# A written-out order for five queues, redone after the planner's count of instructions for a memory step is corrected

## The chip, the cores and the metric

The kernel runs on one core of a Trainium2 chip. Its time is the device time of one execution in microseconds (us); lower is better. The runs shown before the change took 269.98, 270.18 and 270.83 us.

## The reference

The inputs are bf16; sequence 2048, width 512, 32 heads of 16, four segments of 512 tokens, a feed-forward width of 1792.

```
g = sigmoid((x * gate_w).sum(-1))                       # one gate for each token
a: q, k, v = x@wq, x@wk, x@wv ; for each segment s of 512 tokens:
     p     = softmax(q_s k_s^T / 4 + causal mask);  a_dot = p v_s
     a_mem = phi(q_s) M / (phi(q_s) z + 1e-6)           # what earlier segments left
     o_s   = sigmoid(beta) * a_mem + (1 - sigmoid(beta)) * a_dot
     M += phi(k_s)^T v_s ;  z += sum of phi(k_s)        # phi(t) = t+1 if t>0 else exp(t)
   a = o @ wo
b: h = relu(x@W_gate) * (x@W_up);  b = h @ W_down
out = g * a + (1 - g) * b
```

## The kernel before, in words

The program has no loop at run time. A Python object, `Plan`, holds some 1,100 *steps*; each is a handful of instructions on one engine, with the steps it comes after. A list of numbers, `ORDER`, says what stands in each of five queues: TensorE (PE), ScalarE (ACT), VectorE (DVE), GpSimd (POOL) and SyncE's DMA queue (QSP). An entry v means step v//5 on engine v%5, so the list also chooses the engine where a step may run on two. `Plan.lay_out` walks the queues with costs written in the source and emits the steps in the order of the start that it works out. Each engine then runs its queue strictly in order. The same walk hands out the four PSUM banks `rb0`..`rb3`: a step that needs a bank takes the one that is free earliest.

The steps that are spoken of below; the first digit behind a name is the segment (0 to 3), the next a block of 128 columns (eight heads), a fill or a tile of 128 tokens:

- `Q`, `K`, `V` (L492, L518, L535): projections of a segment, four 128x128 by 512 matmuls each (`V` in two halves of 256). `QC`, `KC`, `VC` (L388/L390) bring them out of PSUM. `KO` (L505/L507) is a masked copy of K.
- `QK` (L751): 8 or 16 short matmuls of scores for one of nine fills of a pair of blocks, into `sp`, which has only one buffer. `EX` (L762, ACT): the exponential of it into one of eleven `E` tiles. `MK` (L772, POOL): the causal mask on it. The next `QK` needs the `EX` before it to be done.
- `PV` (L799): 64 short matmuls for one block, into two banks. `TA`, `N0`, `N1`, `N2`, `TB` (L817, L822, L825, L828, L844, all DVE): transpose out of PSUM, normalise, transpose back into `oT`.
- `EK`, `MN`, `PK`, `KX` (L624, L630, L634, L351): phi of K, then a DMA transpose. `MZ` (L648): the *memory visit*, which adds a segment to M and z: 4 groups x 4 tiles x 4 heads = 64 matmuls of 34 columns, each with its weight load. `MA`, `MB` (L658/L660, L666/L669): into the memory matrix. There are three of them.
- `EQ`, `MQ`, `PQ` (L560, L567, L571): phi of Q. `MR` (L694): reading from the memory, 2 or 3 matmuls. `RA`, `RB`, `RC`, `RN` (L704 to L714, DVE): normalise it. `MX` (L351): a DMA transpose into `memT`. `OA` (L850, DVE or POOL): adds `memT` to `oT`.
- `G`, `U` (L910): gate and up projection of 128 columns, four matmuls each; `R` (L922 on ACT, L924 on DVE): relu; `H` (L929, DVE): product.
- `D`, `DB` (L944, L868) and `W` (L957, L876): the two halves of the down projection and the output projection of 128 tokens in one bank, seven, seven and four matmuls. `W` needs all four `OA` of its segment. `OS` and `ST`: scale and store.
- `XT` (L351): x of a segment, transposed by DMA. `VS` (L465): a shifted copy of V, by DMA. The weights wg, wu come in four pieces by DMA (L339).

TensorE runs in four kinds of array split ("full", "rows", "cols", "cols2"); the walk adds `SWITCH` to a step whose kind differs from the one before. It also counts TensorE's instructions. `CODE` holds the count for a kind of step (a matmul is two: weight load and matmul); others are given where the step is made. Each `PAGE` = 256 of them, from `PAGE0` on, the walk lets TensorE wait, if need be, for the next piece of program:

```
for i in (edge - AHEAD, edge):
    if code <= i < code + s.code:
        t = now + cost * (i - code) / s.code
        if i < edge:
            ask = t
        else:
            cost += max(0.0, asked + FETCH - t)
            asked, edge = max(ask, asked + FETCH), edge + PAGE
code += s.code
```

Of the kernel before, what the change touches and what calls it, by code (L numbers as in the profile page):

```python
# [14 lines left out]
D = 512  # L15
# [17 lines left out]
NWARM = 19  # L33
# [5 lines left out]
SWITCH = 0.094  # L39
ENGINES = ('PE', 'ACT', 'DVE', 'POOL', 'QSP')  # L40
ORDER = [
# [60 lines left out]
]  # L102
T0, TU, SPAN, PEN_D, PEN_A, PEN_P = 19.0, 15.6, 4.1, -23.0, 150.0, 146.0


PORT = {'TG', 'RN', 'RC', 'OA', 'KO', 'MB', 'MQ', 'MN', 'GS', 'PQ', 'PK', 'N1', 'N2', 'N3', 'NM'}
CODE = {'WM': 2 * NWARM, 'XP': 4, 'VI': 2, 'YP': 4, 'D': 14, 'DB': 14, 'PV': 128, 'MZ': 96}
PAGE, PAGE0, AHEAD, FETCH = 256, 186, 12, 5.0
PIECE = {'MK': 0.445, 'TL': 0.22, 'ZE': 0.24, 'YL': 0.22, 'MB': 0.3}


# [910 lines left out]
```

## Time and profile before

| | |
|---|---|
| median of three runs | 270.18 us (269.98 to 270.83) |
| profiled execution, its own time | 270.55 us |
| its span in the trace | 268.8 us |
| outside the span | 1.75 us |
| granted TensorE clock | 1.00 |

The page lists how long each engine was busy; the chain of waits goes back from the last instruction to what released it; the timeline lists an engine's instructions with their start, their duration and, in brackets, the idle time ahead of them. A matmul's listed duration overlaps the next one's, so its price is read from starts: the distance from one start to the next.

### The profile page before, as it was taken

The page shows a single profiled execution, that of the slowest core. Times are in us where ns is not written, and L with a number is a line of the kernel's source. Part 1 is how long each engine was busy: PE and PEld are TensorE (multiplying, and loading weights), DVE is VectorE, ACT ScalarE, POOL GpSimd, SP SyncE. Part 2 cuts the span into 40 slices and gives each one's busy share as a digit, 9 for nine tenths or more (in the row PEclk, how much of TensorE's full clock was granted, in tenths as well). Part 3 has the DMA queues.
Part 4 walks back from the last instruction along what each step waited for, and adds up shares of the span by engine and source line. Part 5 has one row for each costly group of instructions (what it writes and reads, how often), then busy time and mean ns, then how long its engine had stood idle before and what let it go on. Part 6 is the DMA issues. An engine that isn't in the chain of part 4 may idle for free.

```text
span 268.8 us, 8007 instructions
## 1 busy us (share of the span) xinstructions
PE 261.6 (97%) x3337; PEld 124.0 (46%) x3337; DVE 187.4 (70%) x460; ACT 188.6 (70%) x180; POOL 146.3 (54%) x322
## 2 busy tenths in 40 slices
PE   7999999999999998999999998999999999999995
PEld 5444345445444444444444444544544454445453
DVE  1798677988975859898881268886975549465901
ACT  3597878899578696798766886879685577755011
POOL 7047764476978535484753637467558434444110
PEclk9999999999999999999999999999999999999999
DMA  6999176130022321102701010110002130010011
GB/s 191 300 260 247 23 196 221 24 79 2 2 44 76 83 42 22 22 20 41 127 4 39 22 41 2 26 36 0 5 0 67 36 84 2 0 22 0 2 32 49
DMA packets 33422, 16.77 MB, mean 62 GB/s; under 512 B 20074, under 2 KB 33386, under 8 KB 33386
## 3 DMA queue, kind: packets, MB, share of 16 engines
q1 hardware_dynamic: 33098, 16.00, 23.5%
q8 instruction: 26, 0.43, 0.7%
q10 hardware_dynamic: 288, 0.26, 0.3%
q14 instruction: 10, 0.08, 0.1%
HBM read 8.26 MB, written 2.10 MB: 39 GB/s over the span
## 4 chain that ended last, share of the span: by engine, by line
PE 90%; DVE 5%; issue 1%; DMA 1%; ACT 1%; DVEq 0%
PE rb L910 33%; PE rb L944 17%; PE rb L492 10%; PE sp L751 9%; PE rb L799 6%; PE rb L957 5%; PE rb L535 4%; PE rb L518 2%; PE rb L868 1%; PE rb L694 1%; DMA xT<-in_A_x_dram 1%; DVE pqT L571 1%; DVE hT L929 1%; ACT E L762 1%; PE rb L405 1%
## 5 line engine op out<-in xcount | busy, mean ns | idle before, releaser
L772 POOL TENSOR_SCALAR_AFFINE_SELECT E<-E 64x256 bf16<-64x256 bf16 x256 | 113.4, 443 | 98.9 <-ACT E L762 87.3
L762 ACT ACTIVATE E<-sp 128x2048 bf16<-128x2048 f32 x72 | 135.1, 1876 | 40.2 <-PE sp L751 35.8
L910 PE MATMUL rb<-xT,wg_sb 128*128 128x512 bf16 x224 | 55.9, 380 | 1.2 <-DVE o L828 1.2
L910 PE MATMUL rb<-xT,wu_sb 128*128 128x512 bf16 x224 | 56.7, 380 | 0.0
L929 DVE TENSOR_TENSOR hT<-rb,rg 128x512 bf16<-128x512 f32 x56 | 37.8, 681 | 16.5 <-PE rb L910 11.6
L944 PE MATMUL rb<-wd_sb,hT 128*128 128x512 bf16 x210 | 49.0, 379 | 0.0
L910 PEld LDWEIGHTS <-wg_sb 128*128 128x128 bf16 x224 | 20.3, 98 | 26.5 <-issue 5.6
L910 PEld LDWEIGHTS <-wu_sb 128*128 128x128 bf16 x224 | 20.4, 98 | 24.6 <-issue 3.5
L751 PE MATMUL sp<-QT,KTo 32*64 32x512 bf16 (+7 forms) x512 | 30.9, 295 | 0.3 <-issue 0.3
L751 PE MATMUL sp<-QT,KT 16*64 16x512 bf16 (+7 forms) x512 | 30.9, 295 | 0.1
L944 PEld LDWEIGHTS <-hT 128*128 128x128 bf16 x210 | 19.7, 98 | 22.7 <-issue 1.8
L922 ACT ACTIVATE rg<-rb 128x512 bf16<-128x512 f32 x31 | 18.5, 597 | 9.3 <-PE rb L910 7.4
L817 DVE STREAM_TRANSPOSE tA<-rb 128x512 f32<-128x512 f32 x32 | 21.0, 690 | 4.3 <-PE rb L799 4.2
L751 PEld LDWEIGHTS <-KT 16*64 16x64 bf16 x512 | 10.8, 102 | 26.4 <-issue 25.7
L924 DVE TENSOR_SCALAR rg<-rb 128x512 bf16<-128x512 f32 x25 | 16.9, 680 | 4.8 <-PE rb L910 4.6
L799 PE MATMUL rb<-E,Vs 64*32 64x448 bf16 (+7 forms) x512 | 18.0, 284 | 0.0
L799 PE MATMUL rb<-E,Vp 64*32 64x448 bf16 (+7 forms) x512 | 17.5, 283 | 0.0
L492 PE MATMUL rb<-xT,wq_sb 128*128 128x512 bf16 x64 | 16.2, 380 | 0.0
L492 PE MATMUL rb<-xT,wk_sb 128*128 128x512 bf16 x64 | 15.7, 380 | 0.0
L957 PE MATMUL rb<-wo_sb,oT 128*128 128x512 bf16 x60 | 15.1, 379 | 0.0
L828 DVE TENSOR_TENSOR o<-tA,co 128x256 bf16<-128x256 f32 x32 | 14.4, 474 | 0.1
L390 DVE CAST KT<-rb 128x512 bf16<-128x512 f32 x10 | 6.9, 689 | 10.8 <-PE rb L492 10.4
(99 smaller groups left out, 296.3 us busy)
## 6 DMA issues: line engine op xcount, KB each, us to landing
out_dram<-osb SPq DMA_DIRECT2D x15, 128.0 KB, 1.7
wd_sb<-in_B_W_down_dram SPq DMA_DIRECT2D x1, 1792.0 KB
wg_sb<-in_B_W_gate_dram SPq DMA_DIRECT2D x3, 512.0 KB, 6.9
wu_sb<-in_B_W_up_dram SPq DMA_DIRECT2D x3, 512.0 KB, 6.8
Vs<-Vp SPq DMA_DIRECT2D x8, 144.0 KB, 2.6
wk_sb<-in_A_wk_dram SPq DMA_DIRECT2D x2, 256.0 KB, 4.5
wq_sb<-in_A_wq_dram SPq DMA_DIRECT2D x2, 256.0 KB, 5.1
wo_sb<-in_A_wo_dram SPq DMA_DIRECT2D x1, 512.0 KB, 8.4
```

Of the source, the lines that this page charges most:

```text
L492: nc.tensor.matmul(rb[s.bank][:], lhsT=w[:, ci, c * P:(c + 1) * P], rhs=xT[i][:, ci, :], start=(ci == 0), stop=(ci == NC - 1))
L751: nc.tensor.matmul(sp[64 * h:64 * h + 64, j, off:off + m], lhsT=kt[32 * j:hi, c0 + w, 64 * ck:64 * ck + 64], rhs=QT[i][32 * j:hi, c0 + w, ...
L762: nc.scalar.activation(Er[n % NE][:], sp[:], ACT.Exp, scale=SCALE)
L772: nc.gpsimd.affine_select(out=v, in_=v, compare_op=ALU.is_ge, fill=0.0, base=0, pattern=[[0, 4], [1, 64]], channel_multiplier=-1)
L799: nc.tensor.matmul(rb[s.banks[h]][32 * j:32 * j + 32, q0:q0 + m], lhsT=v[64 * h:64 * h + 64, ck // 2, o:o + 32], rhs=Er[(base + f) % NE][6 ...
L817: nc.vector.transpose(tA[k].rearrange("p b w -> p (b w)"), rb[a.banks[r]][:])
L910: nc.tensor.matmul(rb[s.bank][:], lhsT=w[:, ci, fv * P:(fv + 1) * P], rhs=xT[i][:, ci, :], start=(ci == 0), stop=(ci == NC - 1))
L922: nc.scalar.activation(rgb[k][:], rb[a.bank][:], ACT.Relu)
L924: nc.vector.tensor_scalar(rgb[k][:], rb[a.bank][:], 0.0, None, ALU.max)
L929: nc.vector.tensor_tensor(hT[:, fv, :], rb[a.bank][:], rgb[k][:], ALU.mult)
L944: nc.tensor.matmul(rb[b][:], lhsT=hT[:, fv, lc:lc + P], rhs=wd_sb[:, fv, :], start=(fv == 0), stop=False)
L957: nc.tensor.matmul(rb[hold.bank][:], lhsT=oT[i][:, ci, lc:lc + P], rhs=wo_sb[:, ci, :], start=False, stop=(ci == NC - 1))
```

## The change

Two lines of constants and the whole of `ORDER`. No step is added or removed and no instruction is written differently.

```diff
-CODE = {'WM': 2 * NWARM, 'XP': 4, 'VI': 2, 'YP': 4, 'D': 14, 'DB': 14, 'PV': 128, 'MZ': 96}
-PAGE, PAGE0, AHEAD, FETCH = 256, 186, 12, 5.0
+CODE = {'WM': 2 * NWARM, 'XP': 4, 'VI': 2, 'YP': 4, 'D': 14, 'DB': 14, 'PV': 128, 'MZ': 128}
+PAGE, PAGE0, AHEAD, FETCH = 256, 188, 6, 4.6
 ORDER = [
-    135, 81, 79, 140, 150, 170, 146, 160, 157, 176, 350, 167, 355, 375, 360, 365, 380, 372, 190, 180, 385, 197, 390,
+    135, 81, 79, 140, 160, 150, 146, 170, 167, 156, 350, 177, 355, 375, 360, 365, 380, 372, 190, 180, 385, 196, 390,
...
```

The constants act on the kernel only through the walk: the order in which the steps are emitted and the banks that they get. `MZ` is now counted with its 128 instructions. The sets of steps on TensorE and on SyncE's queue are the same as before; eight `R`, and one or two steps each of other kinds, stand on another engine (`R`: 31 on ACT and 25 on DVE before, 23 and 33 now; in all ACT has 170 steps for 179, DVE 428 for 420, POOL 95 for 94).

**TensorE, the third memory visit.** Before, `MZ2` (L648) follows the second `PV` (L799) of the first pair of segment 2 at once, and the next scores (L751) follow it:

```order
L799 LDWEIGHTS Vs_108
L799 MATMUL rb_64<-E_110,Vs_108 32x512
L648 LDWEIGHTS pK
L648 MATMUL rb_65<-Vp_106,pK 32x34
...
L751 LDWEIGHTS KT_101
L751 MATMUL sp<-QT_99,KT_101 64x192
```

In the change a `G` (L910) stands behind that `PV`, and `MZ2` behind scores of segment 3, ahead of a down projection (L944):

```order
L799 LDWEIGHTS Vs_108
L799 MATMUL rb_64<-E_110,Vs_108 32x512
L910 LDWEIGHTS wg_sb
L910 MATMUL rb_65<-xT_97,wg_sb 128x512
...
L751 LDWEIGHTS KTo
L751 MATMUL sp<-QT_100,KTo 64x448
L648 LDWEIGHTS pK
L648 MATMUL rb_67<-Vp_106,pK 32x34
...
L944 LDWEIGHTS hT
L944 MATMUL rb_65<-wd_sb,hT 128x512
```

`MZ2` has moved from instruction 4177 of TensorE's queue to 5153, about 1000 instructions later. The second `PV` with `MZ1` and a `QK` behind it stand together in both kernels, but start at instruction 2463 before and 2425 now.

**VectorE, the first pair of segment 0.** Before, from the first transpose out of PSUM (`TA`, L817) on:

```order
L817 STREAM_TRANSPOSE tA_156<-rb_67 128x512
L817 STREAM_TRANSPOSE tA_157<-rb_65 128x512
L822 RECIPROCAL co_158<-tA_156 128x16
L822 RECIPROCAL co_159<-tA_157 128x16
L825 TENSOR_TENSOR co_158<-co_158,Gs_154 128x16
L825 TENSOR_TENSOR co_159<-co_159,Gs_154 128x16
L828 TENSOR_TENSOR o_0_160<-tA_156,co_158 128x16x16
L828 TENSOR_TENSOR o_0_160<-tA_157,co_159 128x16x16
L817 STREAM_TRANSPOSE tA_156<-rb_66 128x512
```

In the change a `PQ` (L571) and an `H` (L929) stand between:

```order
L817 STREAM_TRANSPOSE tA_156<-rb_65 128x512
L817 STREAM_TRANSPOSE tA_157<-rb_67 128x512
L822 RECIPROCAL co_158<-tA_156 128x16
L822 RECIPROCAL co_159<-tA_157 128x16
L825 TENSOR_TENSOR co_158<-co_158,Gs_154 128x16
L571 SCALAR_TENSOR_TENSOR pqT<-QT_100,e1q_141 128x512
L828 TENSOR_TENSOR o_0_160<-tA_156,co_158 128x16x16
L929 TENSOR_TENSOR hT<-rb_67,rg_146 128x512
L817 STREAM_TRANSPOSE tA_156<-rb_64 128x512
```

Between the first `TA` of blocks 0 and 1 and the first `TA` of blocks 2 and 3 of segment 0, VectorE had 38 steps and now has 44: two `PQ`, two `KO`, one each of `R`, `PK`, `MN`, `MQ` and `GS` came in; one `H`, the `MA` and the `MB` went out.

**SyncE's queue, x of segment 3.** Before, the transposing load of x for segment 3 (`XT3`, into `xT_98`) stands between the two `VS`:

```order
L351 DMA_TRANSPOSE pK<-pkT_145 128x4x128
L465 DMA Vs_108<-Vp_106 64x4x288
L351 DMA_TRANSPOSE xT_98<-in_A_x_dram 128x4x512
L465 DMA Vs_108<-Vp_106 64x4x288
L971 DMA out_dram<-osb_150 128x512
```

Now it stands ahead of the last `MX` (`memT`) of segment 1:

```order
L351 DMA_TRANSPOSE memT<-mtok 128x4x128
L351 DMA_TRANSPOSE pK<-pkT_144 128x4x128 x2
L351 DMA_TRANSPOSE xT_98<-in_A_x_dram 128x4x512
L351 DMA_TRANSPOSE memT<-mtok 128x4x128
L465 DMA Vs_108<-Vp_106 64x4x288 x2
```

That `MX` now comes behind a load that is four times its size, and every `W` of segment 1 comes behind it.

118 rows, old and new, of the table ORDER are left out of this document.

## The prediction

> **What bounds the kernel now.** I read the page first, for which engine carries the time: busy shares, the chain of waits, the DMA queues.
>
> ```profile
> PE 261.6 (97%) x3337; PEld 124.0 (46%) x3337; DVE 187.4 (70%) x460; ACT 188.6 (70%) x180; POOL 146.3 (54%) x322
> q8 instruction: 26, 0.43, 0.7%
> PE 90%; DVE 5%; issue 1%; DMA 1%; ACT 1%; DVEq 0%
> ```
>
> TensorE (PE) is busy 97% of the span and 90% of the chain is its own work; the other engines are busy 70% or less. The change leaves TensorE's steps as they are, and I counted the changes of array split on the two orders: 152 in both. So the change can only win what TensorE loses between its matmuls, and can only lose by making it wait. The second line matters for that: TensorE has 3337 matmuls and as many weight loads, 6674 instructions, and queue q8 fetched 26 blocks of program: one for every 257 instructions.
>
> Next the timeline of TensorE, for breaks in its stream. From segment 1 on there are four that are longer than a quarter of a microsecond:
>
> ```profile
> 105.27 0.29 PE L751 MATMUL sp<-QT,KTo 32*64 32x320 bf16 x1
> 106.78 0.39 PE L910 MATMUL rb<-xT,wg_sb 128*128 128x512 bf16 x1 [1.21 <-DVE o L828]
> ...
> 162.14 0.58 PE L648 MATMUL rb<-Vp,pK 128*32 128x34 bf16 x54
> 163.59 0.25 PE L648 MATMUL rb<-Vp,pK 128*32 128x34 bf16 x10 [0.87 <-issue]
> 163.77 0.27 PE L751 MATMUL sp<-QT,KT 16*64 16x192 bf16 x1
> ...
> 191.48 0.27 PE L751 MATMUL sp<-QT,KT 16*64 16x192 bf16 x1
> 192.07 0.24 PE L751 MATMUL sp<-QT,KTo 32*64 32x192 bf16 x1 [0.32 <-issue]
> ...
> 221.78 0.29 PE L751 MATMUL sp<-QT,KT 16*64 16x320 bf16 x1
> 222.07 0.29 PE L751 MATMUL sp<-QT,KTo 32*64 32x320 bf16 x1
> ```
>
> Three fall in the middle of one step, where no step waits for another. How far apart are they? A count of TensorE's matmuls in the stretches from one break to the next:
>
> ```profile
> 106.50:162.60 56.10, 55.70 (x767) 1.00 0.19 39
> 163.50:191.60 28.10, 28.01 (x384) 1.00 0.08 16
> 192.00:221.85 29.85, 29.78 (x384) 1.00 0.17 43
> ```
>
> 768 (767 and one at the edge), 384 and 384 matmuls: 6, 3 and 3 times 128, which is 256 instructions. All four breaks therefore lie on the seams of the blocks that q8 fetches: TensorE waits for its program. The trace puts the first one down to VectorE (L828), but the bank that this L910 takes was free long before: the transposes (L817) that read it last were over at 104.92.
>
> ```profile
> 103.61 1.31 DVE L817 STREAM_TRANSPOSE tA<-rb 128x512 f32<-128x512 f32 x2 [0.53 <-PE rb L799]
> ```
>
> **What the breaks cost.** By starts, with rows of undisturbed steps beside them:
>
> ```profile
> 222.08 0.32 PE L751 MATMUL sp<-QT,KTo 32*64 32x320 bf16 x1
> 222.33 0.39 PE L910 MATMUL rb<-xT,wu_sb 128*128 128x512 bf16 x1
> ...
> 104.53 0.68 PE L648 MATMUL rb<-Vp,pK 128*32 128x34 bf16 x64
> 105.14 0.27 PE L751 MATMUL sp<-QT,KT 16*64 16x192 bf16 x1
> ```
>
> First: 106.78 - 105.27 = 1.51, less the usual 222.33 - 222.08 = 0.25, is 1.26. Second: `MZ2` takes 163.77 - 162.14 = 1.63, `MZ1` 105.14 - 104.53 = 0.61, so 1.02. Third: 0.59. Fourth: 0.29. The sum is **3.16 us**.
>
> The Trainium skill (Runtime: NRT & Kernel Launch, section "Instruction fetch mechanics") says that an engine's program is refilled in blocks of 16 KiB or 256 instructions, and that a crossing is "one DMA tail-bump, mostly hidden". The trace agrees with the block and with "mostly" (22 of 26 show no such break), not with the four. By the Trainium skill alone the change would win nothing; that is a rival below.
>
> **Why they arise, and whether they go.** A block lasts as long as TensorE takes for its 128 matmuls. For the third and the fourth break, the rows in which the block before it began, counting 128 matmuls back:
>
> ```profile
> 189.30 0.25 PE L799 MATMUL rb<-E,Vp 64*32 64x64 bf16 x8
> 218.53 0.25 PE L799 MATMUL rb<-E,Vp 64*32 64x64 bf16 x8
> ```
>
> Both lie in a `PV` (so do the other two). From there to the resumption it took 192.07 - 189.30 = 2.8 and 222.07 - 218.53 = 3.5 us; the other two lie between. So the next block is there 2.8 to 3.5 us after the present one was entered, and a block that is worked off sooner ends in a break. Only `PV`, `MZ` and `QK` are that dense. The plan before counted each `MZ` 32 instructions short, so that its seams slid off the real ones after each visit; all four breaks come after the first visit.
>
> In the changed order I counted the seams from the same phase and priced the blocks with these starts:
>
> ```profile
> 13.90 1.90 PE L910 MATMUL rb<-xT,wg_sb 128*128 128x512 bf16 x8
> 15.64 1.03 PE L910 MATMUL rb<-xT,wu_sb 128*128 128x512 bf16 x4
> 16.60 0.24 PE L751 MATMUL sp<-QT,KT 16*64 16x128 bf16 x1
> 102.37 0.21 PE L799 MATMUL rb<-E,Vs 64*32 64x64 bf16 x4
> ```
>
> A full matmul is (15.64 - 13.90)/8 = 0.217; a `QK` 0.38 (105.14 to 105.27 and the usual 0.25), with 0.09 for the change of split ahead of it (16.60 - 15.64 - 4 x 0.217); a pair of `PV` 104.53 - 102.37 = 2.16, some 1.0 and 1.16. The shortest block of the new order ends in the second `PV` of segment 3: ten full matmuls, one `QK`, a whole `PV` and 38 of 64 matmuls of the next: 2.17 + 0.47 + 1.0 + 0.69 = 4.3 us. The next shortest, at a `PV` of segment 0 and one of segment 1, come to 4.5 and 4.7 in the same way. `MZ2` stands alone, far from any `PV`; the group with `MZ1` has moved by 38 instructions, so that its second seam falls behind the scores into projections. 4.3 is above 3.5: **all four breaks go, -3.16**. Were a fetch 4.6 us late, as the plan assumes, two short breaks would stay, 0.3 + 0.1 = 0.4.
>
> **What the new order may cost.** *VectorE in segment 0.* The densest stretch of VectorE, from the first `PV` of segment 0 to its third:
>
> ```profile
> 44.90:65.00 20.10, 20.10 (x352) 9.42 (x344) 17.94 (x45) 17.45 (x17) 11.34 (x25) 1.00 0.16 35
> ...
> L571 DVE SCALAR_TENSOR_TENSOR pqT<-QT,e1q 128x512 bf16<-128x512 bf16 x12 | 8.6, 716 | 1.0 <-POOL e1q L567 1.0
> L507 DVE TENSOR_SCALAR KTo<-KT,mcol_o 128x512 bf16<-128x512 bf16 x9 | 3.6, 404 | 0.1
> L924 DVE TENSOR_SCALAR rg<-rb 128x512 bf16<-128x512 f32 x25 | 16.9, 680 | 4.8 <-PE rb L910 4.6
> 53.06 1.09 DVE L666 TENSOR_TENSOR mem<-mzacc,bdm 128x128 bf16<-128x128 f32 x4
> 54.08 0.39 DVE L669 TENSOR_TENSOR mem<-mzacc,bdm 128x32 bf16<-128x32 f32 x1
> ```
>
> Its third number is VectorE: 17.94 busy of 20.10. In come two `PQ` and a `PK`, the same operation on the same shape, 3 x 0.716 = 2.15; two `KO`, and `MQ` and `MN`, which are of `KO`'s kind and shape, 4 x 0.404 = 1.62; an `R` 0.68: 4.45. Out go the `MB`, 1.09 + 0.39, and an `H`, which is as long as the `R`: 2.16. `GS` and `MA`, one short step each, I set off against each other. Net +2.3, against 20.10 - 17.94 = 2.2 of idle time: VectorE is full there. Queued behind it are steps that give banks back (`TA`, `H`, `VC`, `KC`), and TensorE waits for those. It costs between 0, if all of it fits into the idle time, and 2.3, if none does. I take **+0.5**, nearer the lower end: idle time and addition all but cancel, and TensorE has three other banks to work on while one is late; but a queue without gaps cannot make up for a late product.
>
> *Steps that change the engine.* Eight `R` go from ACT to VectorE, 8 x 0.68 = 5.4 us of its 187.4. Outside the stretch above VectorE has room (70% busy over the span), and ACT gets shorter: 0, in the worst case a rival below.
>
> *SyncE's queue.* `XT3` now stands ahead of the last `MX` of segment 1.
>
> ```profile
> 128.99 3.06 SPq L351 DMA_TRANSPOSE xT<-in_A_x_dram  x1
> DMA to landing us min/median/max: 2.4/2.4/4.4
> L850 POOL TENSOR_TENSOR oT<-oT,memT x6: 1154/1157/1382, 117.2 to 256.0; 128x512 bf16<-128x512 bf16 x6
> ```
>
> `XT3` may start after the last `U` of segment 1; then 3.06 on the queue, at most 4.4 for the `MX` (second row), two `OA` on POOL at 1.38: 10.2 us, until the first `W` of segment 1. TensorE has 42 matmuls of `D` and `DB` (9.1) and four `QK` (1.9) in between: 11.0. Cost 0, bounded by 0.5 for a mask that POOL does first. Where this cover is gone, `W` waits for the excess, us for us.
>
> *The rest.* The weight pieces are asked for in another order, but their first readers are moved with them; head and tail have the same steps, and the last `W` is again behind the last block's chain. 0, bounded by 0.3 either way.
>
> **Sum.** Against the profiled execution's own 270.55: -3.16 + 0.5 = 267.9. The median of the runs, 270.18, lies 0.37 lower: **267.5 us**. About 0.3% (0.8 us) is what a measurement of this kernel can tell from no change.
>
> **Rivals.** (1) *The stretch costs its upper end*: VectorE gives banks back late, +2.3 in place of 0.5: 269.7, on the runs' scale 269.3. For it: VectorE is full there. Against: nearly as full before, without a wait. Chance 0.17, split evenly between faster and same. (2) *The breaks are not fetches, or come back at other seams*: 270.2, give or take 0.8. For it: the trace puts one break down to VectorE. The Trainium skill's sentence on the crossing (Runtime: NRT & Kernel Launch, "Instruction fetch mechanics") speaks for it too. Against: distances of exactly 128 matmuls. Chance 0.08, nearly all same. (3) *Slower: VectorE becomes the bound.* If of the 5.4 us of moved `R` nothing fits beside other work, TensorE waits for their banks and the time is 270.55 - 3.16 + 5.4 = 272.8, or 272.4; it decides from 4.0 us on (3.16 and the 0.8), three quarters of it. Against: VectorE is idle for 30% of the span, and many of the moved steps are not near a full stretch. Chance 0.12. The forecast has 0.63, with a range of its own from 266.5 to 268.7.
>
> The range: 266.4 is all breaks gone, no cost and 0.6 of small waits gained; upwards it takes in rival 1 and most of rival 2: 270.0. Faster: 0.63 + 0.09 + 0.03 = 0.75; slower 0.12; same 0.13.
>
> **What would show it.** Right: no idle time of 0.3 us or more put down to "issue" in `MZ`, `PV` or `QK` of PE, and 128-matmul blocks of 4.3 us and more; PE's busy share up by a point. The second step is wrong if breaks of 0.3 us or more recur at multiples of 128 matmuls; the VectorE term if TensorE waits for L817, L929 or L390 between 46 and 68 us by more than 2 us; the SyncE term if a `W` (L957) waits for L850 near 140. The forecast fails if TensorE's waits outside the seams grow by over 2.4 us.

## The result, and the profile after

The changed kernel takes 267.94 us (median of six runs, 267.33 to 268.09), the kernel before 270.36 us beside it (six runs, 269.98 to 270.83). The ratio is 0.9905, with a 95% interval of 0.989 to 0.992: faster by 2.4 us. The forecast was 267.5 us. The profiled execution of the changed kernel took 267.33 us, its span 265.6 us.

The page of the changed kernel, busy times and the chain's shares:

```profile
PE 257.4 (97%) x3298; PEld 123.1 (46%) x3337; DVE 195.3 (74%) x468; ACT 183.9 (69%) x171; POOL 150.6 (57%) x323
PE 96%; issue 2%; DMA 1%; DVE 0%; DVEq 0%
```

VectorE is busier by 7.9 us and ScalarE less busy by 4.7, in the direction of the moved steps, and TensorE still carries the chain. This trace holds 3298 of TensorE's 3337 matmuls (all weight loads are there), so the busy time of PE cannot be compared to the tenth, and some gaps are only missing records. The table of TensorE's waits has to be read with that:

```profile
PE rb L395 <- DVE zeros L267: 1.0, 1, 1.0
PE rb L799 <- issue: 0.9, 1, 0.9
PE rb L944 <- issue: 0.6, 4, 0.2
PE rb L957 <- issue: 0.3, 2, 0.2
```

The two lower rows are gaps of 0.2 us where a full matmul's record is missing; they do not recur in the profiles of this kernel that have all records. The second row is a real break, and a new one. The four of before are gone. In TensorE's timeline (start, duration, engine, line, operation, and in brackets the idle time ahead), the `MZ1` with the `QK` behind it, then `MZ2` at its new place:

```profile
101.60 0.68 PE L648 MATMUL rb<-Vp,pK 128*32 128x34 bf16 x64
102.21 0.27 PE L751 MATMUL sp<-QT,KT 16*64 16x192 bf16 x1
...
102.34 0.29 PE L751 MATMUL sp<-QT,KTo 32*64 32x320 bf16 x1
102.57 1.68 PE L910 MATMUL rb<-xT,wu_sb 128*128 128x512 bf16 x6
...
203.04 0.67 PE L648 MATMUL rb<-Vp,pK 128*32 128x34 bf16 x64
```

From the last score matmul to the next projection (here of `U`) it is 0.23 us, where before it was 1.51, and `MZ2` runs in one piece of 64 where before it was 54, a break, and 10.

The new break lies in the second `PV` of segment 0 (`PV01`, in the first pair):

```profile
42.10 1.90 PE L910 MATMUL rb<-xT,wu_sb 128*128 128x512 bf16 x8
...
46.38 0.39 PE L799 MATMUL rb<-E,Vs 64*32 64x256 bf16 x8
46.50 0.30 PE L799 MATMUL rb<-E,Vp 64*32 64x320 bf16 x1
47.70 0.35 PE L799 MATMUL rb<-E,Vp 64*32 64x320 bf16 x7 [0.91 <-issue]
47.73 0.52 PE L799 MATMUL rb<-E,Vs 64*32 64x384 bf16 x8
```

By starts it lasts 47.70 - 46.50 = 1.2 us, again in the middle of a step. Its price is 1.1 us: from 46.50 to the next row it is 1.23, and 0.14 in the undisturbed step that experiment 3 shows (46.75 to 46.89). Counted back from it, 128 matmuls begin with the second of the eight at 42.10, at about 42.3: a seam once more. But this block lasted 4.2 us, and the next one came 5.4 us after it was entered, not 2.8 to 3.5. Two views suggest why. The DMA queues in two stretches, from the seam to 45.2 and from there on (queue, packets, megabytes, time as a share of 16 engines):

```profile
q1 hardware_dynamic: 1035, 1.06, 107.5%
...
q1 hardware_dynamic: 475, 0.47, 103.9%
q8 instruction: 1, 0.02, 4.2%
```

In the first stretch q8 moves nothing and the engines are full with q1; the program's packet is first seen in the second, 2.9 us after the seam. In the third break of before it was seen at 189.4, 0.1 us after its block was entered at 189.30. From that packet to the resumption it is about the same in both, 2.5 us here (45.2 to 47.70) and 2.7 there (to 192.07). So what is late here lies ahead of the packet. What fills the engines stands in SyncE's timeline, after and before:

```profile
39.20 0.58 SPq L339 DMA_DIRECT2D wd_sb<-in_B_W_down_dram  x1
39.84 0.82 SPq L339 DMA_DIRECT2D wo_sb<-in_A_wo_dram  x1
```

```profile
36.05 0.57 SPq L339 DMA_DIRECT2D wd_sb<-in_B_W_down_dram  x1
36.68 0.83 SPq L339 DMA_DIRECT2D wo_sb<-in_A_wo_dram  x1
```

The load of W_down and wo (2.3 MB) now starts 3.15 us later. It stands behind the fourth `KX` of segment 0 as it did, but that `KX` comes later, and so the load runs over the fetch that this dense block needs.

**Where the 3.22 us between the two profiled executions went** (270.55 to 267.33): four breaks gone, -3.16; the new one, +1.1; TensorE comes to its first K projection at 8.04 in place of 9.10, -1.06; all else together -0.1.

### The profile page after: what moved, and what is told of

The parts are those of the page before. It is cut to its first block, busy times and chain, and to the rows that moved or that the text cites. A ratio compares the mean times of both kernels' runs of the same rounds, so it can differ in the third digit from the quotient of the medians.

```text
span 265.6 us, 7948 instructions
## 1 busy us (share of the span) xinstructions
PE 257.4 (97%) x3298; PEld 123.1 (46%) x3337; DVE 195.3 (74%) x468; ACT 183.9 (69%) x171; POOL 150.6 (57%) x323
## 4 chain that ended last, share of the span: by engine, by line
PE 96%; issue 2%; DMA 1%; DVE 0%; DVEq 0%
PE rb L910 37%; PE rb L944 17%; PE rb L492 11%; PE sp L751 10%; PE rb L799 7%; PE rb L957 5%; PE rb L535 4%; PE rb L518 2%; PE rb L694 1%; PE rb L868 1%; DMA xT<-in_A_x_dram 1%; PE rb L648 1%; PE rb L405 1%; PE rb L876 0%; DVE rg L887 0%
## 5 line engine op out<-in xcount | busy, mean ns | idle before, releaser
L772 POOL TENSOR_SCALAR_AFFINE_SELECT E<-E 64x256 bf16<-64x256 bf16 x256 | 115.1, 450 | 85.7 <-ACT E L762 73.0
L910 PE MATMUL rb<-xT,wg_sb 128*128 128x512 bf16 x217 | 56.0, 380 | 0.5 <-issue 0.2
L910 PE MATMUL rb<-xT,wu_sb 128*128 128x512 bf16 x207 | 54.0, 380 | 0.9 <-issue 0.2
L929 DVE TENSOR_TENSOR hT<-rb,rg 128x512 bf16<-128x512 f32 x56 | 38.2, 684 | 16.0 <-PE rb L910 12.2
L944 PE MATMUL rb<-wd_sb,hT 128*128 128x512 bf16 x201 | 47.5, 379 | 0.9 <-issue 0.6
L910 PEld LDWEIGHTS <-wg_sb 128*128 128x128 bf16 x224 | 20.5, 98 | 25.3 <-issue 4.3
L910 PEld LDWEIGHTS <-wu_sb 128*128 128x128 bf16 x224 | 20.3, 98 | 24.3 <-issue 3.7
L944 PEld LDWEIGHTS <-hT 128*128 128x128 bf16 x210 | 19.6, 98 | 23.4 <-issue 2.0
L751 PE MATMUL sp<-QT,KT 16*64 16x512 bf16 (+7 forms) x512 | 30.3, 295 | 0.1
L751 PE MATMUL sp<-QT,KTo 32*64 32x512 bf16 (+7 forms) x512 | 30.3, 295 | 0.0
L924 DVE TENSOR_SCALAR rg<-rb 128x512 bf16<-128x512 f32 x33 | 22.6, 684 | 10.1 <-PE rb L910 9.6
L817 DVE STREAM_TRANSPOSE tA<-rb 128x512 f32<-128x512 f32 x32 | 21.2, 692 | 6.5 <-PE rb L799 6.5
L751 PEld LDWEIGHTS <-KT 16*64 16x64 bf16 x512 | 10.5, 102 | 26.7 <-issue 26.2
L922 ACT ACTIVATE rg<-rb 128x512 bf16<-128x512 f32 x23 | 13.7, 597 | 8.2 <-PE rb L910 7.0
L799 PE MATMUL rb<-E,Vp 64*32 64x448 bf16 (+7 forms) x512 | 17.7, 284 | 0.9 <-issue 0.9
L799 PE MATMUL rb<-E,Vs 64*32 64x448 bf16 (+7 forms) x512 | 18.2, 284 | 0.0
L535 PE MATMUL rb<-wv_sb,xT 128*128 128x257 bf16 (+1 forms) x96 | 14.5, 273 | 0.0
L828 DVE TENSOR_TENSOR o<-tA,co 128x256 bf16<-128x256 f32 x32 | 14.3, 464 | 0.1
```

The source lines that it names most:

```text
L535: nc.tensor.matmul(rb[s.bank][:, 0:n], lhsT=xT[i][:, ci, t * P:(t + 1) * P], rhs=wv_sb[:, ci, h * D // 2:h * D // 2 + n], start=(ci == 0), ...
L751: nc.tensor.matmul(sp[64 * h:64 * h + 64, j, off:off + m], lhsT=kt[32 * j:hi, c0 + w, 64 * ck:64 * ck + 64], rhs=QT[i][32 * j:hi, c0 + w, ...
L772: nc.gpsimd.affine_select(out=v, in_=v, compare_op=ALU.is_ge, fill=0.0, base=0, pattern=[[0, 4], [1, 64]], channel_multiplier=-1)
L799: nc.tensor.matmul(rb[s.banks[h]][32 * j:32 * j + 32, q0:q0 + m], lhsT=v[64 * h:64 * h + 64, ck // 2, o:o + 32], rhs=Er[(base + f) % NE][6 ...
L817: nc.vector.transpose(tA[k].rearrange("p b w -> p (b w)"), rb[a.banks[r]][:])
L910: nc.tensor.matmul(rb[s.bank][:], lhsT=w[:, ci, fv * P:(fv + 1) * P], rhs=xT[i][:, ci, :], start=(ci == 0), stop=(ci == NC - 1))
```

## The experiments

**Theory A**: the breaks are waits for program blocks, at every 128th matmul, and the order only decides what lies at a seam. **Rival B**: they are waits of the steps themselves (a bank, VectorE), which the new order removes. The two are told apart by moving the seams while the order stays.

**1. before_seams_moved.** The warm-up ahead of all work gets 96 matmuls more, short ones:

```diff
-            for k in range(n):
+            for k in range(4):
                 nc.tensor.matmul(rb[3][:, 0:P], lhsT=zeros[:], rhs=zeros[:], start=True, stop=True)
+            for k in range(111):
+                nc.tensor.matmul(rb[3][:, 0:16], lhsT=zeros[:], rhs=zeros[:, 0:16], start=True, stop=True)
```

> The kernel before with its order untouched; only the warm-up at the head has 115 matmuls (4 of 128 columns and 111 of 16) in place of 19, so that every seam of the 256-instruction blocks falls 96 matmuls earlier in the work. The warm-up computes nothing that is used. Theory A (TensorE waits for its program at seams that come less than about 3.5 us apart): priced with the starts of undisturbed steps, the short blocks are now one of 2.4 us in a PV of segment 1 and two of 3.0 and 3.2; the breaks at 105, 162, 191 and 221 us go, and about 1.0 us of breaks is left in place of 3.2: 268.2 us, 0.992 of before. Theory B (the four breaks are waits for other engines, which the new order removed): the same breaks, 270.3 us, 1.00.

Measured: 268.79 us against 270.64 for the kernel before beside it, ratio 0.9935 (0.9911 to 0.9958). All of TensorE's waits, and the place of the largest break of before:

```profile
PE rb L395 <- DVE zeros L267: 1.0, 1, 1.0
...
106.40 0.29 PE L753 MATMUL sp<-QT,KTo 32*64 32x320 bf16 x1
106.63 1.04 PE L912 MATMUL rb<-xT,wg_sb 128*128 128x512 bf16 x4
```

(Line numbers are two higher here.) With the order of before, step for step, none of the four is left; L912 follows after 0.23 us though VectorE does what it did, so the releaser L828 in the trace of before was wrong. The gain is 1.85 and not 3.16 because the longer warm-up costs at the start: the first K projection begins at 10.27, not 9.10. From there to the last `W` the kernel is 2.8 us shorter than before. A holds for the four, B falls.

One part of the expectation failed: of the short blocks at the moved seams, 1.0 us of breaks should have been left, and there is none. Counted on in steps of 128, these blocks are worked off in 2.1 (from 102.8), 3.1 and 3.1 us. Before the first of them the packet of q8 was seen at 102.2, 0.6 us ahead of the seam. In before, too, a block of 2.5 us (from 65.1) ends without a break, its packet seen at the seam. So the count of 128 tells where a break can come; the working-off time alone does not tell whether it comes. What lets a fetch begin earlier is not shown. The time of 268.79 is near the expected 268.2 in part by luck: the missing breaks and the later start pull opposite ways.

**2. after_seams_moved.** The same in the changed kernel, 40 matmuls more (14 long, 45 short). This puts seams of the new order back into dense places:

> The changed kernel with its order untouched; the warm-up has 59 matmuls (14 of 128 columns and 45 of 16) in place of 19, so that every seam falls 40 matmuls earlier in the work. Theory A: blocks of 2.3 us (first scores after the second PV pair of segment 0), 1.8 us (MZ1), 3.1 us and 2.2 us (behind the PV pairs of segment 2) come up, with breaks of about 0.9, 1.4, 0.1 and 1.0 us: 3.4 us in all, 271.3 us or 1.003 of before (270.5 to 272.5, since the break of 1.2 us at 46.5 us may grow or go). Theory B: the time of the changed kernel, 267.9 us, 0.991 of before.

Measured: 270.57 us, ratio to the kernel before 1.0002 (0.9984 to 1.0019): the whole gain is gone. TensorE's waits and three of the four places:

```profile
PE sp L753 <- issue: 1.3, 2, 0.8
PE rb L650 <- issue: 1.2, 1, 1.2
...
68.68 0.32 PE L753 MATMUL sp<-QT,KT 16*64 16x384 bf16 x1
69.44 0.32 PE L753 MATMUL sp<-QT,KTo 32*64 32x384 bf16 x1 [0.44 <-issue]
...
101.92 0.62 PE L650 MATMUL rb<-Vp,pK 128*32 128x34 bf16 x58
103.77 0.22 PE L650 MATMUL rb<-Vp,pK 128*32 128x34 bf16 x6 [1.24 <-issue]
...
194.59 0.27 PE L753 MATMUL sp<-QT,KT 16*64 16x192 bf16 x1
195.67 0.27 PE L753 MATMUL sp<-QT,KTo 32*64 32x192 bf16 x1 [0.82 <-issue]
```

Less the usual distances these are 0.78, 1.39 and 1.08; a fourth of 0.29 lies at 163.8: 3.5 us, at the four steps that the count of 128 gave, while the break in `PV01`, whose seam has moved away, is gone. The first K projection begins at 8.72, 0.7 us later, for the longer warm-up. +3.5 - 1.1 + 0.7 = 3.1, against 2.9 between the two profiled executions (270.19 and 267.33). So the new order is not free of breaks by itself: how many it has depends on the phase of the seams.

All these breaks lie at one phase. Counted from a profile's first matmul, those of before come behind 1375, 2142, 2526 and 2910 matmuls, those here behind 862, 1374, 2142 and 2526, and that in `PV01` behind 478 (in the repeats of experiment 4, which hold all records): each is 94 or 95 more than a multiple of 128.

What the constants do: with the new ones and the old `ORDER` the five queues hold the same instructions as before, one for one, with the same banks. With the new `ORDER` the old constants would give other banks to 132 of TensorE's 357 steps; that was not run, so what the constants are worth beside the `ORDER` that was drawn up with them is open.

**3. after_wd_early.** Is the new break the load's doing? In the changed kernel the load of W_down and wo goes ahead of the fourth `KX` of segment 0: its two entries of `ORDER` move forward, and it waits for three `PK` in place of four.

```diff
             if seg == 0:
                 for w in ("wd", "wo"):
-                    ld[w].after += st[0]["PK"]
+                    ld[w].after += st[0]["PK"][:3]
```

Only SyncE's queue changes, and this is the place:

```
 L351 DMA_TRANSPOSE pK<-pkT_144 128x4x128 x2
-L351 DMA_TRANSPOSE pK<-pkT_145 128x4x128
 L339 DMA wd_sb<-in_B_W_down_dram 128x14x512
 L339 DMA wo_sb<-in_A_wo_dram 128x4x512
+L351 DMA_TRANSPOSE pK<-pkT_145 128x4x128
```

> The changed kernel; on SyncE's queue the loads of W_down and wo (2.3 MB) stand one place earlier, ahead of the fourth transpose of phi(K) of segment 0, whose data they no longer wait for; all other queues are the same. In the changed kernel they were issued at 39.2 us and moved data until 47.5 us; here they should be issued at about 30.5 and be over by 39. Theory A with a fetch that queues behind bulk data: the one break left, 1.2 us in the second PV of segment 0 at 46.5 us, goes, and the time is 266.7 us, 0.987 of before. Rival (that break is VectorE being full in this stretch, as the prediction's term had it): it stays, 267.9 us, 0.991.

Measured: **266.48 us** (266.41 to 266.9), ratio to before 0.9845 (0.9822 to 0.9868): 1.5 us faster than the changed kernel, and faster than both. The loads' issue, the step in which the break was, and TensorE's waits:

```profile
30.50 0.58 SPq L339 DMA_DIRECT2D wd_sb<-in_B_W_down_dram  x1
31.14 0.91 SPq L339 DMA_DIRECT2D wo_sb<-in_A_wo_dram  x1
...
46.75 0.44 PE L799 MATMUL rb<-E,Vp 64*32 64x320 bf16 x8
46.89 0.49 PE L799 MATMUL rb<-E,Vs 64*32 64x384 bf16 x8
...
PE rb L395 <- DVE zeros L267: 1.0, 1, 1.0
PE rb L518 <- DMA wv_sb<-in_A_wv_dram: 0.2, 1, 0.2
```

The same block, at the same seam, worked off in the same 4.2 us, now ends without a wait, and its packet is seen at 42.9, 0.3 us after the seam. The rival that VectorE, full in this stretch, made the break would have left it and the 267.9 us. The load in flight made that fetch late; that the packet queued behind the load's packets, and not behind something else that the load does, is read from the order of the two in the trace, not tried. Nor does every fetch during this load come as late: in before the packet of the block entered at 42.9 is seen 1.0 us after the seam, some 0.2 us before the load's last packets, and that block (3.4 us) ends without a break.

**4. Repeats for the start.** The first K projection began 1.06 us earlier in the profile after, though TensorE has the same instructions up to there in both (three transposes of x stand in another order, and SyncE's queue differs from 7.4 us on). Of the 1.06, x landing sooner gives 0.46 (first transpose, L405, at 3.40 for 3.86) and the six V projections behind it 0.6: before, they start 0.43 us apart to the last, after, the last three 0.22. Two profiles more of each kernel, before and after by turns:

> The kernel before, unchanged, for a second profile of its head. In the profiles so far the first K projection starts at 9.1 us before and about 1.05 us earlier in the changed kernel. If the new order makes the head shorter, this start lies at 9.1 again (within 0.2); if it is chance of one execution (when x lands, when the clock rises), it lies anywhere between 8 and 9.1.

> The changed kernel, unchanged. Order: the first K projection at 8.1 us again (within 0.2). Chance: anywhere between 8 and 9.1. The break in the second PV of segment 0 (1.2 us at 46.5) is there again in both cases.

> As the first repetition of the kernel before: 9.1 us if it is the order, 8 to 9.1 if it is chance.

> As the first repetition of the changed kernel: 8.1 us if it is the order, 8 to 9.1 if it is chance; the break at 46.5 us again.

Measured: first K at 9.08 and 9.10 for before (single times 271.82 and 272.92), at 8.18 and 8.57 for the changed kernel (267.69 and 268.28). The break in `PV01` was there both times, 1.45 and 1.66 us by starts. Neither expectation fits whole: before repeats its 9.1, the changed kernel spreads by 0.5 but stays below it. The two executions of before are 1.3 and 2.4 us slower than that of its first profile, and have waits that no profile of the changed kernel has: `V` of segment 3 waits 0.8 us for x in both, and a K projection 1.0 us at 28 us in the second. What such waits add to the gain of the medians is not known.

**5. Four tries at the start's cause**, each timed: the first dozen entries of `ORDER` exchanged between the two kernels (they order three of x's transposes and their copies), and the idle time ahead of the landing of x taken away from before and given to the changed kernel. The two latter have this edit, with 256 or 64 columns for the last six of 19 warm-up matmuls:

```diff
-                nc.tensor.matmul(rb[3][:, 0:P], lhsT=zeros[:], rhs=zeros[:], start=True, stop=True)
+                w = P if k < 13 else 256
+                nc.tensor.matmul(rb[3][:, 0:w], lhsT=zeros[:, 0:P], rhs=zeros[:, 0:w], start=True, stop=True)
```

> The kernel before with the first dozen entries of ORDER as the changed kernel has them. The five queues hold the same instructions as before, so by theory A (the order of the head's steps does nothing; the start of TensorE's clock differs from run to run) the median is 270.3 us, within 0.4, and the first K projection starts somewhere between 8.0 and 9.2 us. By theory B (those entries make the changed kernel's head 0.5 to 1 us shorter) it starts at 8.0 to 8.6 and the time is 269.6.

> The changed kernel with the first dozen entries of ORDER as before. The five queues hold the same instructions as in the changed kernel: theory A, 267.9 us and the first K projection between 8.0 and 9.2 us; theory B, the first K at 9.1 and 268.7 us. The break in the first PV (PV01) should be there again, 1.2 to 1.7 us.

> The kernel before with the last six of its 19 warm-up matmuls 256 columns wide in place of 128: same number of instructions, so the same seams, but TensorE is not idle for 0.3 to 0.6 us before x lands. If that idle time is what holds the half-rate clock until 7.2 us in the kernel before, the six first V matmuls take 2.0 us in place of 2.7, the first K starts at 8.2 to 8.6 and the time is 269.7. If it is not, the first K starts at 9.1 or, where the warm-up outlasts the landing of x, up to 0.3 later, and the time is 270.3 to 270.6.

> The changed kernel with the last six warm-up matmuls 64 columns wide in place of 128: TensorE is idle for some 0.6 us before x lands, as in the profile of the kernel before. If that idle time holds the half-rate clock longer, the first K starts at 9.1 and the time is 268.6; if not, at 8.0 to 8.6 and 267.9.

Measured, beside 271.02 for before on that chip: 271.37 (ratio 1.0007, 0.9973 to 1.0041), 268.39 (0.9897, 0.982 to 0.9974), 271.12 (1.0003, 0.9973 to 1.0034) and 267.89 (0.9875, 0.9811 to 0.9939). The entries do nothing that shows (first K at 8.93 and 8.29, each within or near its own kernel's spread). The start of before with the long warm-up, and of the changed kernel with the short one, by their timelines; the last row of the first group is from the table on the wq weights:

```profile
4.63 1.96 PE L519 MATMUL rb<-wv_sb,xT 128*128 128x512 bf16 x6
8.43 3.04 PE L493 MATMUL rb<-xT,wk_sb 128*128 128x512 bf16 x11
13.49 0.21 PE L752 MATMUL sp<-QT,KT 16*64 16x64 bf16 x1
...
DMA wq_sb<-in_A_wq_dram: 0.6, 1
```

```profile
3.47 1.03 PE L406 MATMUL rb<-ident,xT 128*128 128x128 bf16 x8 [0.55 <-DMA xT<-in_A_x_dram]
4.33 2.24 PE L519 MATMUL rb<-wv_sb,xT 128*128 128x512 bf16 x6
8.34 0.81 PE L493 MATMUL rb<-xT,wk_sb 128*128 128x512 bf16 x3
```

Without idle time, before's first K came at 8.43, as expected, but the first `QK` came at 13.49 where it had come at 13.55: the Q projections waited 0.6 us for wq, so nothing was won. With idle time, the changed kernel still had its first K at 8.34 and the same time. The expected mechanism therefore fails on this side: the idle time alone does not decide the start, as far as one profile of each can tell. The break in `PV01` is in both profiles of the changed kernel here. Why all profiles of the changed kernel come to the first K sooner stays open.

## Why the prediction was right, and where it was off

*The breaks are fetches at seams (step one).* Right: experiments 1 and 2 show from both sides that they lie at the seams, and q8's packet is seen 2.3 to 2.9 us before TensorE goes on, in each break of before and of experiment 2. Rival 2, that they are not fetches, is refuted; its second half, that they come back at other seams, came true for one of them, by a cause it did not name.

*All four go, -3.16, since no block is shorter than 4.3 us.* The four went, but a break of over 0.3 us in a `PV` at a multiple of 128 is what the prediction named as the sign that this step is wrong. The failing term is the limit of 3.5 us: it came from fetches in a stretch without bulk loads, and was carried over to segment 0, where the weights still come in. The block there that was put at 4.5 us took 4.2, and its fetch 5.4 in place of 3.5. (The block forecast as the shortest, 4.3 us in segment 3, took 4.0, and had no break.) The net gain was 3.16 - 1.1 = 2.1. The 0.4 us that the text kept for a fetch of 4.6 us was the right kind of worry and too small: the fetch's time depends on the DMA traffic and is no constant even without it (2.2 us or less in experiment 1, 3.5 in the fourth break of before). SyncE's queue was read in detail around segment 1 for x, and dismissed for the weights in one sentence ("The rest"); the load of W_down, which now came later, belonged there and was not looked at.

The Trainium skill (Runtime: NRT & Kernel Launch, section "Instruction fetch mechanics") calls a crossing "mostly hidden". The runs agree in number (20-odd of 26 show no break) and not in price: the same order costs 268.79 or 270.64, and the same changed order 267.94 or 270.57, by where the crossings lie.

*VectorE's stretch, +0.5 (bounds 0 to 2.3).* Too high: 0 as far as the trace shows. TensorE's waits in the changed kernel between 46 and 68 us are one row, the break. The second row is the stretch from the first `PV` to the third again (TensorE's busy time is the second number, VectorE's the fourth):

```profile
PE rb L799 <- issue: 0.9, 1, 0.9
...
45.15:66.87 21.72, 20.66 (x309) 9.86 (x305) 19.11 (x46) 19.19 (x22) 15.27 (x33) 1.00 0.29 80
```

VectorE is busy 19.1 us in place of 17.9, and between the two `TA` that the sum was counted between, 19.6 in place of 17.7: +1.9 of the +2.3 did come in. But the stretch holds more of TensorE's work as well (20.7 us for 20.1), since a memory visit went out and projections and scores came in. In experiment 3, without the break, it lasts 20.6 us, VectorE is busy 19.0 of them, and TensorE does not wait for it. The step that failed is "VectorE full, so TensorE waits": here the engine was 92% busy at no cost. Rival 1, the upper end, falls with it.

*Eight `R` on VectorE, 0; rival 3, slower.* Right: VectorE is busy 195.3 us in place of 187.4, and in this profile no wait of TensorE names it after the first microsecond.

*SyncE's queue, x ahead of the last `MX`, 0.* Right: no `W` waits for L850. x starts at 129.60 and the `MX` at 133.51:

```profile
129.60 1.90 SPq L351 DMA_TRANSPOSE xT<-in_A_x_dram  x1
133.51 1.19 SPq L351 DMA_TRANSPOSE memT<-mtok  x1
```

*Head and tail, 0 within 0.3.* Wrong for the head, by -1.06 in the two profiles and by -0.5 to -0.9 between the repeats of experiment 4. By luck it made up for most of the break that the prediction missed, so the total came out nearer than its terms. How much of it is in the medians is not known, since each profile shows one execution.

*The scale.* The prediction turned the profiled scale into the median's by subtracting 0.37. The profiled execution of before lay 0.19 above its median in the end (270.36), that of the changed kernel 0.61 below its own. So the sum on the profiled scale, 267.9, was 0.6 too high, and the forecast of the median, 267.5, 0.4 too low.

## What to carry to other kernels

Where an engine is over 95% busy and still has short breaks in the middle of steps, count instructions between them: distances that are multiples of one number, here 128 matmuls, point to the program's own delivery, whatever releaser the trace names, and a few padding instructions at the start are a cheap test, since they move every seam and no step. An order that is laid against such seams holds for one phase and for the DMA traffic of that moment only. When bulk loads move in a queue, look what else of the DMA engines' work falls into the window: here 3 us later cost a third of the gain, and 8.7 us earlier brought it back.

## What the hardware showed that was not expected

In the breaks, the time from entering a block to having the next was 2.8 to 3.5 us where the DMA engines were quiet, and 5.4 to 5.8 us in three profiles with a 2.3 MB load in flight; experiment 1 had one block followed after 2.2 us. Six equal V projections at the start, behind the same instructions, took from 1.96 to 2.94 us in different profiles (the longest with a pause of some 0.3 us between two of them), 0.43 us a matmul for a longer or shorter while. The Trainium skill (TensorE: Matmul & The Clock Gate, Part 1) has the full clock depend on a free-running window of activity, so that the number of slow matmuls differs from run to run; the spread here agrees, and that it leans to one kernel is not explained by it.
